# A second Strassen level for three products of the first GEMM: what it does to a TensorE-bound kernel

## The chip, the cores and the metric

The kernel runs on one core of a Trainium2 chip. The metric is the device time of one execution in microseconds (us); smaller is better. The kernel before measured 664.18 us (median of three runs, 664.06 to 664.48). A 2% rule decides "faster", "same" and "slower". A program on one core has no second die to compare with.

## The reference

A retention layer, an ELU and two matrix products, all in float32:

```python
state = gamma[None, :, None, None] * state + np.einsum('bhd,bhe->bhde', k[:, :, t], v[:, :, t])
y[:, :, t] = scale * np.einsum('bhd,bhde->bhe', q[:, :, t], state)
# ... y (4 x 8 heads x 768 x 64) becomes x, 3072 tokens x 512
h = x @ w_in                                             # 512 -> 2048, "first GEMM"
g = np.where(h > 0.0, h, np.exp(np.minimum(h, 0.0)) - 1.0)   # ELU
return (g @ w_out).astype(np.float32)                    # 2048 -> 512, "second GEMM"
```

## The kernel before

The 3072 tokens go through in six blocks of 512. Block 0 uses plain GEMMs. Blocks 1 to 5 use Strassen's algorithm: seven products M1 to M7 in place of eight. The first GEMM runs it for each of four quarters n of the output rows, and the products are summed in PSUM banks a, b and d. From block 2 on, the second GEMM has a second Strassen level: each of its seven products is again made of seven small ones ("a quadruple" gives four output quarters). Between the products of the second GEMM stand bursts of small 64x64 matmuls: the retention of the next block.

The ELU of a 128x512 tile is two ScalarE (ACT) instructions and one VectorE (DVE) instruction. The DVE part is put off until the next ELU is issued:

```python
def elu(g, h):
    r = epool.tile([P, 512], FP32, name="r", tag="r")
    nc.scalar.activation(r, h, AF.Relu, scale=-1.0)
    nc.scalar.activation(r, r, AF.Exp, scale=-1.0)
    flush()                                    # the DVE ends still put off
    later.append(lambda: nc.vector.scalar_tensor_tensor(g, r, -1.0, h, ALU.add, ALU.max))

def strassen(product, use, between):           # one quarter of the first GEMM
    # ...
    pa = bank("a");  product(1, pa, True);  m1 = kept(pa)          # kept: copy on ACT
    yield
    pb = bank("b");  product(2, pb, True);  use("C11", plus(pb, m1))   # plus: sum on DVE
    yield
    product(6, pa, False);  u2 = kept(pa)
    yield
    pd = bank("d");  product(7, pd, True)
    yield
    product(5, pa, False);  u4 = kept(pa);  use("C22", plus(pd, u4))
    yield "gap"
    product(3, pa, False);  use("C12", pa)
    yield
    product(4, pd, False);  h = plus(pd, u2)
    yield "last"
    use("C21", h)
```

The second GEMM's second level follows the same pattern with 128 columns. Two things in it matter later: `copy` is on ACT, `add` on DVE, and in the traces both engines work through their instructions in the order in which they are issued (in the trace of after, ACT starts the copy of a product whose slot ended at 277.78 us only at 280.44, behind two ELUs issued ahead of it; in that of e1_elus_behind, DVE stands idle for 1.46 us in front of one sum, and the sums behind it come later; both are shown below):

```python
def inner(j):                                  # one product of the second GEMM
    # ...
    pa = bank("a")[:, 0, 0:P];  product(j, 1, pa, True);  m1 = copy(pa)
    pb = bank("b")[:, 0, 0:P];  product(j, 2, pb, True);  add(res[:, 0, 0], pb, m1)
    yield
    product(j, 6, pa, False);  u2 = copy(pa)
    pd = bank("d")[:, 0, 0:P];  product(j, 7, pd, True)
    yield
    product(j, 5, pa, False);  add(res[:, 1, 1], pd, copy(pa))
    # ... products 3 and 4
```

Of the kernel before, what the change touches and what calls it, by code (L numbers as in the profile page):

```python
# [2 lines left out]

# [5 lines left out]
FP32 = mybir.dt.float32  # L9
# [7 lines left out]
def kernel(  # L17
# [3 lines left out]
    w_bits: bass.AP,  # L21
    scratch: bass.AP,
    scratch2: bass.AP,
    out: bass.AP,
    dims,
):



# [74 lines left out]



    w_a = [const.tile([P, 2, 2, 2, P], FP32, name=f"w_a{n}") for n in range(NQ)]
    w_b = [const.tile([P, 2, 2, 2, P], FP32, name=f"w_b{n}") for n in range(NQ)]
    w_s = [const.tile([P, 3, 2, 2, P], FP32, name=f"w_s{n}") for n in range(NQ)]
    NPIECE = 2 * NQ + NF  # L110
    staged, prepared, decoded = [], [], []

# [109 lines left out]


    xb = const.tile([P, 4, TB], FP32, name="xb")
    xt = [const.tile([P, 2, TH], FP32, name=f"xt{n}") for n in range(4)]
    carry = [const.tile([P, HP, D], FP32, name=f"carry{n}") for n in range(2)]
    held = {}

# [138 lines left out]
        while later:  # L367
            later.pop(0)()

    def elu(g, h):  # L370

        r = epool.tile([P, 512], FP32, name="r", tag="r")
        nc.scalar.activation(r, h, AF.Relu, scale=-1.0)  # L373
        nc.scalar.activation(r, r, AF.Exp, scale=-1.0)  # L374
        flush()
        later.append(lambda: nc.vector.scalar_tensor_tensor(g, r, -1.0, h, ALU.add, ALU.max))  # L376

    def plain_first():

# [167 lines left out]
                scratch2[j - 1, :, 1024 * k : 1024 * k + 1024], x.rearrange("p k f d -> p (k f d)")  # L547
            )

    def second(tb):  # L550
        def product(j, ps, begin):
            ws = fetched.pop((tb, j))
            for f in range(NF):
                for d in range(2):
                    nc.tensor.matmul(  # L555
                        ps[:, d, :], lhsT=ws[:, 2 * d + f // 4, f % 4, :], rhs=gq[INPUT2[j]][:, f, :],
                        start=(begin and f == 0 and d == 0), stop=(f == NF - 1), skip_group_check=True,
                    )
            at = ORDER2.index(j) + 3
            if j in (2, 6):  # L560
                next_input(j)
            combine_w_out(j, ws)
            if at < 7:
                fetch(tb, ORDER2[at])

        def use(name, h):
            r, t = int(name[1]) - 1, int(name[2]) - 1
            if name == "C12":
                ot = hpool.tile([P, 2, TH], FP32, name="h", tag="h")
                nc.scalar.copy(ot, h)  # L570
                h = ot
            nc.sync.dma_start(out[tb, r, t].rearrange("p d c -> p (d c)"), h.rearrange("p d c -> p (d c)"))

        return strassen(product, use, None)
# [1 line left out]


    RING = 11
    USE = [(1, k) for k in (1, 2, 6, 7, 5)]
    for at in range(1, 7):  # L580
        j, before = ORDER2[at], ORDER2[at - 1]
        USE += [(j, 1), (j, 2), (before, 3), (before, 4), (j, 6), (j, 7), (j, 5)]
    USE += [(4, 3), (4, 4)]
    to_fetch = [(tb, j, k) for tb in range(2, NTB) for j, k in USE]
    small_w = []

    def fetch_small():
        if not to_fetch:
            return
        tb, j, k = to_fetch.pop(0)  # L590
        t = ring.tile([P, 4, P], FP32, name="wq", tag="wq")
        if k in (1, 2, 4):
            q = 4 * SLOT[j] + {1: 0, 2: 1, 4: 3}[k]
            nc.sync.dma_start(t.rearrange("p f d -> p (f d)"), scratch[q])
        else:
            n = {5: 0, 6: 1, 7: 2, 3: 3}[k]
            nc.sync.dma_start(t.rearrange("p f d -> p (f d)"), scratch2[j - 1, :, 512 * n : 512 * n + 512])
        small_w.append(((tb, j, k), t))

    def second_twice(tb, behind_last):  # L600
        quarter = lambda x, r, t: x[:, 4 * r : 4 * r + 4, P * t : P * t + P]
        ts, kept2 = {}, {}

        def inputs(j):
            x, t = gq[INPUT2[j]], tpool.tile([P, 4, 4, P], FP32, name="ts", tag="ts")
            b11, b12, b21, b22 = (quarter(x, a, b) for a in range(2) for b in range(2))
            sub = lambda o, x, y: nc.vector.tensor_tensor(out=o, in0=x, in1=y, op=ALU.subtract)
            sub(t[:, 0], b12, b11)
            sub(t[:, 1], b22, t[:, 0])
            sub(t[:, 2], b22, b12)  # L610
            sub(t[:, 3], b21, t[:, 1])
            ts[j] = {1: b11, 2: b21, 3: b22, 4: t[:, 3], 5: t[:, 0], 6: t[:, 1], 7: t[:, 2]}

        def product(j, k, ps, begin):
            name, w = small_w.pop(0)
            assert name == (tb, j, k)
            for f in range(4):
                nc.tensor.matmul(  # L618
                    ps, lhsT=w[:, f, :], rhs=ts[j][k][:, f, :], start=(begin and f == 0), stop=(f == 3),
                    skip_group_check=True,  # L620
                )
            fetch_small()
# [9 lines left out]
        def inner(j):  # L632
            pool, tag = (mpool, "m") if j in (1, 6, 7, 5) else (hpool, "h")
            res = pool.tile([P, 2, 2, P], FP32, name="res", tag=tag)
            pa = bank("a")[:, 0, 0:P]
            product(j, 1, pa, True)
            m1 = copy(pa)
            pb = bank("b")[:, 0, 0:P]
            product(j, 2, pb, True)
            add(res[:, 0, 0], pb, m1)  # L640
            yield
            product(j, 6, pa, False)
            u2 = copy(pa)
            pd = bank("d")[:, 0, 0:P]
            product(j, 7, pd, True)
            yield
            product(j, 5, pa, False)
            add(res[:, 1, 1], pd, copy(pa))
            yield
            product(j, 3, pa, False)  # L650
            nc.scalar.copy(res[:, 0, 1], pa)
            product(j, 4, pd, False)
            add(res[:, 1, 0], pd, u2)
            sum_up(j, res.rearrange("p d t c -> p (d t c)"))
# [23 lines left out]
                add(m, kept2[7], m)  # L678
                store("C21", m)

        inputs(1)
        before = iter(())
        for at, j in enumerate(ORDER2):
            cur = inner(j)
            next(cur)
            if j == 1:
                yield "tail"
            for _ in before:
                pass
            if j == 2:  # L690
                next_input(2)
            if j == 5:
                next_input(6)
            if j == 1:

                next(cur)
                yield "elu"
                next(cur)
            if at + 1 < 7:
                inputs(ORDER2[at + 1])  # L700
            else:
                behind_last()
            if j != 1:
                next(cur)
                next(cur)
            before = cur
            yield j
        for _ in before:
            pass


    prepare(2)
# [51 lines left out]
            for _ in combine_w_in(0):  # L764
                pass
    combine_x()
    for j in ORDER2[:3]:
        fetch(1, j)


    def retention_step(tb, step):
# [8 lines left out]
        elif step < 5:  # L780
            outputs_step(tb, step - 2)

    tail = iter(())
    for tb in range(1, NTB):
        more = tb + 1 < NTB
        for n in range(NQ):
            cur = first(n)
            for at in range(3):
                next(cur)

            for _ in tail:
                pass
            side = combine_w_in(n + 1) if tb == 1 and n + 1 < NQ else iter(())
            for s in cur:
                next(side, None)
                if s == "gap":
                    break
            for _ in side:
                pass
            tail = cur  # L800
            if more:
                load((tb + 1) * CPB + n)
                scale_v((tb + 1) * CPB + n)
        if tb == 1:
            cur = second(tb)
            next(cur)
            next(cur)
            for _ in tail:
                pass
            flush()  # L810
            for step, s in enumerate(cur):
                retention_step(tb + 1, step)
            combine_x()
            tail = iter(())
            early.close()
            ring = ctx.enter_context(tc.tile_pool(name="ring", bufs=RING))
            tpool = ctx.enter_context(tc.tile_pool(name="tpool", bufs=2))
            for _ in range(RING):
                fetch_small()
        else:  # L820
            cur = second_twice(tb, combine_x if more else lambda: None)
            next(cur)
            for s in tail:
                if s == "last":
                    break
            next(cur)
            for _ in tail:
                pass
            flush()
            for step, j in enumerate(cur):  # L830

                if step > 0:
                    retention_step(tb + 1, step - 1)
                if j == ORDER2[-1]:
                    break
            tail = cur
    for _ in tail:
        pass

# [45 lines left out]
```

## Time and profile before

| | before |
|---|---|
| time, median of 3 | 664.18 us |
| span of the profiled run | 658.9 us |
| PE (TensorE) busy | 637.3 us, 97% |
| DVE / ACT / POOL busy | 66% / 35% / 4% |
| one product of 256 columns, start to start | 1.727 us |
| one product of 128 columns, start to start | 0.893 us |
| one token block (2 to 5), start to start | 102.65 us |

The profile counts an engine as busy from an instruction's start to its end. Matmuls overlap (a product of 256 columns is shown 1.89 us long, and the next starts 1.727 us after it), so for TensorE the distance from one start to the next says more than the busy time. One more view names the limit: the chain of work that ended last, followed back through the run. Its first line gives the share of the span that each engine has in it:

```profile
PE 95%; DVE 2%; DMA 1%; issue 1%; SPq 0%; ACT 0%; DVEq 0%
```

TensorE has 95% of the chain. No other engine delays it for long.

### The profile page before, as it was taken

The page shows a single profiled execution, that of the slowest core. Times are in us where ns is not written, and L with a number is a line of the kernel's source. Part 1 is how long each engine was busy: PE and PEld are TensorE (multiplying, and loading weights), DVE is VectorE, ACT ScalarE, POOL GpSimd, SP SyncE. Part 2 cuts the span into 40 slices and gives each one's busy share as a digit, 9 for nine tenths or more (in the row PEclk, how much of TensorE's full clock was granted, in tenths as well). Part 3 has the DMA queues.
Part 4 walks back from the last instruction along what each step waited for, and adds up shares of the span by engine and source line. Part 5 has one row for each costly group of instructions (what it writes and reads, how often), then busy time and mean ns, then how long its engine had stood idle before and what let it go on. Part 6 is the DMA issues. An engine that isn't in the chain of part 4 may idle for free.

```text
span 658.9 us, 14662 instructions
## 1 busy us (share of the span) xinstructions
PE 637.3 (97%) x6144; PEld 537.5 (82%) x6144; DVE 434.7 (66%) x769; ACT 228.3 (35%) x432; POOL 23.8 (4%) x28
## 2 busy tenths in 40 slices
PE   4799999999999999999999999999999999999997
PEld 4664445458888888889999889999889999888996
DVE  5798688566757644549856457867447958355974
ACT  7477542014431002543112554111455111445211
POOL 1000100001100000200000200000100000000000
PEclk9999999999999999999999999999999999999999
DMA  8658977549114757605767703777801768200693
GB/s 342 235 166 289 343 228 232 143 133 376 72 65 160 255 211 257 254 1 174 223 206 254 251 1 95 228 228 253 301 2 42 242 206 267 96 1 20 222 305 126
DMA packets 63825, 123.64 MB, mean 188 GB/s; under 512 B 5136, under 2 KB 22544, under 8 KB 61712
## 3 DMA queue, kind: packets, MB, share of 16 engines
q1 hardware_dynamic: 63760, 122.70, 55.6%
q8 instruction: 49, 0.80, 0.5%
q14 instruction: 16, 0.13, 0.1%
HBM read 100.66 MB, written 22.02 MB: 186 GB/s over the span
## 4 chain that ended last, share of the span: by engine, by line
PE 95%; DVE 2%; DMA 1%; issue 1%; SPq 0%; ACT 0%; DVEq 0%
PE pa L497 21%; PE pa L618 15%; PE pd L497 10%; PE pd L618 8%; PE hp L396 6%; PE pb L497 5%; PE pa L410 4%; PE pa L555 4%; PE pb L618 4%; PE pd L555 2%; PE kv L287 2%; PE pb L410 2%; PE pd L410 2%; PE y L335 2%; PE sc L265 2%; PE y L311 2%
## 5 line engine op out<-in xcount | busy, mean ns | idle before, releaser
L452 DVE TENSOR_TENSOR h<-pd,m 128x512 f32<-128x512 f32 x42 | 29.1, 692 | 86.1 <-ACT m L447 68.6
L447 ACT COPY m<-pa 128x512 f32<-128x512 f32 x63 | 36.3, 577 | 109.7 <-PE pa L497 73.7
L626 ACT COPY ms<-pa 128x128 f32<-128x128 f32 x84 | 22.3, 265 | 125.3 <-PE pa L618 122.3
L374 ACT ACTIVATE r<-r 128x512 f32<-128x512 f32 x96 | 60.5, 630 | 3.0
L618 PE MATMUL pd<-ts,wq 128*128 128x128 f32 x448 | 59.9, 277 | 0.3 <-DVE res L630 0.3
L618 PE MATMUL pa<-ts,wq 128*128 128x128 f32 x448 | 59.2, 275 | 0.0
L373 ACT ACTIVATE r<-h 128x512 f32<-128x512 f32 x60 | 37.9, 631 | 57.2 <-DVE h L452 57.2
L618 PEld LDWEIGHTS pd<-ts,wq 128*128 128x128 f32 x448 | 54.5, 192 | 1.2 <-DVE res L630 0.9
L618 PEld LDWEIGHTS pa<-ts,wq 128*128 128x128 f32 x448 | 54.8, 192 | 0.2
L618 PE MATMUL pa<-gC,wq 128*128 128x128 f32 x384 | 52.0, 278 | 0.4 <-ACT ms L626 0.4
L376 DVE SCALAR_TENSOR_TENSOR gC<-r,h 128x512 f32<-128x512 f32 x60 | 42.1, 701 | 11.3 <-ACT r L374 11.3
L618 PEld LDWEIGHTS pa<-gC,wq 128*128 128x128 f32 x384 | 47.2, 192 | 1.7 <-ACT ms L626 0.5
L239 POOL TENSOR_TENSOR kvn<-kvn,vf 128x512 f32<-128x512 f32 x20 | 21.8, 1089 | 455.7 <-DMA kvn<-in_qkv_dram 455.7
L497 PE MATMUL pa<-xb,w_s 128*128 128x256 f32 x160 | 37.8, 379 | 0.0
L497 PE MATMUL pa<-xb,w_a 128*128 128x256 f32 x160 | 37.8, 379 | 0.0
L497 PE MATMUL pa<-xt,w_s 128*128 128x256 f32 x160 | 37.8, 379 | 0.0
L497 PE MATMUL pb<-xb,w_a 128*128 128x256 f32 x160 | 37.8, 379 | 0.0
L497 PE MATMUL pd<-xt,w_s 128*128 128x256 f32 x160 | 37.8, 379 | 0.0
L497 PE MATMUL pa<-xt,w_b 128*128 128x256 f32 x160 | 37.8, 379 | 0.0
L497 PE MATMUL pd<-xt,w_b 128*128 128x256 f32 x160 | 37.8, 379 | 0.0
L630 DVE TENSOR_TENSOR res<-pd,ms 128x128 f32<-128x128 f32 x56 | 16.1, 287 | 28.8 <-PE pd L618 26.3
L497 PEld LDWEIGHTS pb<-xb,w_a 128*128 128x128 f32 x160 | 30.4, 190 | 4.1
(121 smaller groups left out, 1092.7 us busy)
## 6 DMA issues: line engine op xcount, KB each, us to landing
wq<-scratch_dram SPq DMA_DIRECT2D x196, 256.0 KB, 4.0
wraw<-in_w_dram SPq DMA_DIRECT2D x16, 1024.0 KB, 6.0
qk<-in_qkv_dram SPq DMA_DIRECT2D x24, 512.0 KB, 8.7
kvn<-in_qkv_dram SPq DMA_DIRECT2D x24, 512.0 KB, 9.4
scratch_dram<-so SPq DMA_DIRECT2D x22, 512.0 KB, 3.4
ws<-scratch_dram SPq DMA_DIRECT2D x7, 1024.0 KB, 7.0
scratch_dram<-w_s SPq DMA_DIRECT2D x8, 512.0 KB, 7.3
out_dram<-res SPq DMA_DIRECT2D x12, 256.0 KB, 3.4
```

Source lines behind the costliest of these rows:

```text
L239: eng.tensor_tensor(out=kv[:, 1], in0=kv[:, 1], in1=vf[:, i].unsqueeze(2).to_broadcast([C, H, D]), op=ALU.mult)
L373: nc.scalar.activation(r, h, AF.Relu, scale=-1.0)
L374: nc.scalar.activation(r, r, AF.Exp, scale=-1.0)
L376: later.append(lambda: nc.vector.scalar_tensor_tensor(g, r, -1.0, h, ALU.add, ALU.max))
L396: nc.tensor.matmul(hp, lhsT=w[n][:, fi, j // 2, j % 2, :], rhs=xb[:, j, :], start=(j == 0), stop=(j == 3))
L410: nc.tensor.matmul(ops[d], lhsT=wo[:, row, d * P : (d + 1) * P], rhs=g_plain[row * NF + f], start=(f == 0 and row == 0), stop=(f == NF - 1 ...
L447: nc.scalar.copy(m, ps)
L452: nc.vector.tensor_tensor(out=h, in0=ps, in1=m, op=ALU.add)
L497: nc.tensor.matmul(ps[:, fi, :], lhsT=w[:, fi, j2, :], rhs=x[:, j2, :], start=(begin and fi == 0 and j2 == 0), stop=(j2 == 1), skip_group_ ...
L555: nc.tensor.matmul(ps[:, d, :], lhsT=ws[:, 2 * d + f // 4, f % 4, :], rhs=gq[INPUT2[j]][:, f, :], start=(begin and f == 0 and d == 0), sto ...
L618: nc.tensor.matmul(ps, lhsT=w[:, f, :], rhs=ts[j][k][:, f, :], start=(begin and f == 0), stop=(f == 3), skip_group_check=True,)
L626: nc.scalar.copy(m, ps)
```

## The change

In blocks 2 to 5 the products M2, M3 and M7 of the first GEMM are taken over all four quarters at once and split by a second Strassen level: 3 x 7 small products of 128 columns replace 3 x 4 products of 256. The intent is to save TensorE work. M1 of all four quarters comes in front, then M2, M3 and M7 with their small products, then M6, M5 and M4 of the quarters. A sum is taken on DVE right behind its product, and the DVE ends of up to three ELUs may be put off, so that they come between. The new weight combinations are made once on POOL in block 1 and go to DRAM. The core of the diff (cuts marked with ..., comments added here):

```diff
-    def elu(g, h):
+    def elu(g, h, depth=1, then=None):
-        r = epool.tile([P, 512], FP32, name="r", tag="r")
+        r = epool.tile([P, 512], FP32, name="r", tag="r", bufs=3)
...
-        flush()
-        later.append(lambda: nc.vector.scalar_tensor_tensor(g, r, -1.0, h, ALU.add, ALU.max))
+        while len(later) >= depth:
+            later.pop(0)()
+        later.append(last)
...
+    def combine_small(j):
+        t = stage.tile([P, 4, 4, P], FP32, name="wi", tag="stage")
...
+        tt = lambda o, x, y, op: nc.gpsimd.tensor_tensor(out=o, in0=x, in1=y, op=op)
+        tt(s1, a21, a22, ALU.add)
+        tt(s2, s1, a11, ALU.subtract)
+        tt(s3, a11, a21, ALU.subtract)
+        tt(s4, a12, s2, ALU.subtract)
+        nc.sync.dma_start(scratch3[j - 1], t.rearrange("p k f d -> p (k f d)"))
...
+    def first_twice(tb, j):
...
+        pa = full(bank("a"))
+        product(1, pa, True)
+        m1 = lift(pa)                        # copy on ACT
+        yield
+        pb = full(bank("b"))
+        product(2, pb, True)
+        plus(0, 0, pb, m1)                   # sum on DVE
+        product(6, pa, False)
+        u2 = lift(pa)
+        pd = full(bank("d"))
+        product(7, pd, True)
+        m7 = lift(pd)
+        yield
+        product(5, pa, False)
+        plus(1, 1, pa, m7)
...
+        for at, j in enumerate(TWICE):           # TWICE = [2, 3, 7]
+            cur = first_twice(tb, j)
+            next(cur)
+            next(tail, None)
+            if at == 2:
+                first_end(1, "C11", qa[1])()     # sum on DVE, ELU on ACT
+                first_end(2, "C11", qa[2])()
+            next(cur)
+            for _ in tail:
+                pass
+            if at > 0:
+                pop()
+                first_end((0, 0, 3)[at], "C11", qa[(0, 0, 3)[at]])()
...
+        order = (6, 0), (6, 1), (5, 0), (4, 0), (5, 1), (6, 2), (4, 1), (6, 3), (5, 2), (4, 2), (5, 3)
...
+        next(sec)                            # products 1 and 2 of the second GEMM, and their sum
+        pop()
+        ends.pop(0)()
+        part(4, 3)                           # M4 of quarter 3, and the C21 sum
+        pop()
+        next(sec)                            # products 6 and 7
+        ends.pop(0)()
+        flush()
```

## The prediction

> **What bounds the kernel now.** I read the page's busy shares first, then the waits of PE, then PE's order of time, then stretches by stage.
>
> ```profile
> PE 637.3 (97%) x6144; PEld 537.5 (82%) x6144; DVE 434.7 (66%) x769; ACT 228.3 (35%) x432; POOL 23.8 (4%) x28
> ```
>
> ```profile
> PE sc L265 <- DMA qk<-in_qkv_dram: 8.9, 2, 7.5
> PE pa L385 <- DVE xb L342: 2.8, 2, 1.4
> ```
>
> PE is busy 97% of the span. Its two largest waits lie before the first 40 us are over, where this change does nothing. To learn what a busy PE is worth I took starts, not durations:
>
> ```profile
> 293.04 1.89 PE L497 MATMUL pd<-xt,w_s 128*128 128x256 f32 x8
> 294.76 1.89 PE L497 MATMUL pa<-xt,w_b 128*128 128x256 f32 x8
> ...
> 305.46 1.06 PE L618 MATMUL pb<-gC,wq 128*128 128x128 f32 x8
> 306.35 1.06 PE L618 MATMUL pa<-gC,wq 128*128 128x128 f32 x8
> ```
>
> Each row is one product of four written matmuls (two records each). A product with 256 columns starts 1.727 us before the next (several rows averaged), one with 128 columns 0.893 us. So half the columns cost 0.893/1.727 = 0.517, not 0.5.
>
> ```profile
> 353.25:399.20 45.95, 45.95 (x223) 40.68 (x222) 21.28 (x34) 22.15 (x39) 4.49 (x4) 1.00 0.40 137
> 399.20:455.90 56.70, 55.76 (x877) 54.12 (x876) 44.96 (x89) 11.42 (x34) 0.00 (x0) 1.00 0.68 211
> ```
>
> These are the first and second half of one token block (columns: stretch, PE, weight loads, DVE, ACT, POOL, clock, DMA share, GB/s). In the first GEMM PE never stops, while DVE and ACT are less than half busy. A block has 28 first-GEMM products x 1.727 = 48.4 us, 49 second-GEMM products x 0.893 = 43.8 us, and some 10.5 us of retention: 102.7 us, and the blocks start 102.65 us apart. There is nothing left to save but PE work.
>
> [...] A record here takes 1.727/8 = 216 ns and 0.893/8 = 112 ns[...]. [...] a product that accumulates on a bank must wait until the copy out of that bank is done. The trace before shows such a wait bare, with nothing put between:
>
> ```profile
> 651.28 1.06 PE L618 MATMUL pa<-ts,wq 128*128 128x128 f32 x8
> 652.37 0.27 ACT L626 COPY ms<-pa 128x128 f32<-128x128 f32 x1 [1.52 <-PE pa L618]
> 652.69 1.16 PE L618 MATMUL pa<-gC,wq 128*128 128x128 f32 x8 [0.35 <-ACT ms L626]
> ```
>
> The product's slot ends at 651.28 + 0.89 = 652.17; ACT starts 0.20 later; PE starts 0.05 after ACT ends. [...] Before, a DVE operation beside a running POOL one took 0.84 instead of 0.68 us: too little to count.
>
> **The change part by part.** In the four blocks 2 to 5, M2, M3 and M7 of the first GEMM (over all four quarters n) become 7 products of 4 small matmuls each.
> - Removed per block: 12 products x 1.727 = 20.72 us. Added: 3 x 7 x 0.893 = 18.76 us. PE gains 1.97 us per block, 7.9 us in all. Records of PE rise from 6144 to 6144 + 4 x 3 x (56 - 32) = 6432. This is a floor: 664.2 - 7.9 = 656.3 if PE stays as dense.
> - DVE gets 100 more operations (built program: 871 against 771): sums land by addition in their place instead of accumulating in PSUM, plus input combinations. A 128x512 operation is followed after 0.60 us when independent, 0.71 when it needs the one before. Some 17 of 0.60 and 8 small ones make about +12 us of DVE per block: off the path on average (66% busy), not locally.
> - ACT has 434 instructions as before, in another order. POOL gets 12 operations of about 1.09 us (13 us, once, in block 1) for new weight combinations, which go to DRAM and come back as 48 more ring tiles of 256 KB. The ring is 11 deep, the first-GEMM stage had a DMA share of 0.40, and no weight wait of PE exists before: hidden. In block 1 the second GEMM's first 1 MB weight tile is now fetched only behind that POOL work; from 166 us (end of the weight combinations on DVE) + 13 + 7 (landing of such a tile) it is there at 186, needed at 190.7. Near, but hidden; I allow 0.5 us.
>
> **New waits, worked out by hand from the orders of the engines.** Set 0 at the start of a block; the small products of M2, M3, M7 follow four 1.727 products and two left over.
> (a) During M7, PE must wait at its fifth product until ACT has copied the third out of the same bank. ACT stands in order behind two whole ELUs (quarters 1 and 2 of C11), and these behind the ELU of quarter 0. Chain: the last product of M2 ends at 18.52; +0.20 copy starts, +0.58; DVE sum 0.03 + 0.69; ACT Relu and Exp 0.04 + 0.66 + 0.63; DVE ELU end 0.04 + 0.60, a PSUM sum 0.60, the sum of quarter 1 0.69; ACT 0.04 + 0.66 + 0.54 + 0.66 + 0.54, then the copy 0.57 and 0.05 to PE: 26.3. PE is there at 24.77 (7 more products of 0.893). It waits 1.6 us.
> (b) At the end of M7 the seventh product follows after 0.89 us a DVE read (0.20 + 0.69 + 0.05): 0.05.
> (c) The twelve large products M6, M5, M4 take 20.7 us; DVE has about 37 operations of 0.60 to 0.71 there, some 23 to 24 us including the products of the second GEMM put between. It keeps up until C21 of quarter 3: its sum starts at about 23.1 on that stage's clock and the second GEMM's product on the same bank is due at 23.4: wait 0.4. Behind it the second GEMM's second input needs the last ELU end at about 26.9, when PE arrives at 26.5, but only for its third matmul: nearly nothing.
> Sum of waits 2.0 per block, 8.0 in four; 664.2 - 7.9 + 8.0 + 0.5 = 664.8. But every wait of this sum is a difference of close times, the waits can only be got wrong to the small side in (c), and a few tenths less in each step of (a), which has eleven, would halve it. I take 1.4 per block: 664.2 - 7.9 + 5.6 + 0.5 = 662.4.
>
> **Rivals.**
> - *The work shows in full.* PE stays dense and all waits hide behind neighbours: 656 to 657. For it: before, no ELU delays PE at all, and the change plainly orders sums to avoid waits. Against it: the ACT order in (a), where 2.4 us of ELUs stand directly ahead of a copy with only two small products (1.79 us) to cover it.
> - *DVE becomes the bound of M6, M5, M4.* If its operations cost 0.69 instead of 0.60 each there (many depend on the one before), 37 x 0.09 = 3.3 us more per block reach PE as waits on banks and on the second GEMM's inputs: 4 x 3.3 = 13 us, so 676. Against: runs of independent operations are seen at 0.60, and DVE waits for PE several times in that stage, which absorbs some.
> - *Weights come late* (ring or first 1 MB tiles): a few us once, 665 to 668. Against: slack of some 5 us and the low DMA share.
>
> **Range and chances.** The floor of 656.3 is firm, since the product times are measured. Upwards, (a) and (c) in full plus a late weight tile give 668. Central 662.4, eight in ten within 657 to 667.5. Over 2% faster means below 651: impossible but for an unseen saving. Over 2% slower means above 677: the whole of the DVE rival.
>
> **What would show it right or wrong.** Right: 6432 PE records, PE busy near 630 us, one wait of PE on ACT's 128x512 copy in each of four blocks of over 1 us, inside the M7 products and behind two Relu/Exp pairs; a smaller wait on DVE at the pd bank where the second GEMM begins. First GEMM stage of a block shorter than before by less than 1 us. Wrong: no PE wait on ACT (then 656 to 658), or PE waits all through the M6/M5/M4 stage on DVE (then 670 and more), or small products in the first GEMM starting further apart than 0.893 us, which would take away the gain at its root.

## The result, and the profile after

The changed kernel measured 672.51 us (median of 4 runs, 671.29 to 673.75), the kernel before 664.33 beside it. All ratios here are the mean time of one kernel's fast runs over that of the other's in the same rounds, so they are not quite the ratios of the quoted medians. This one is 1.0109, with a 95% interval of 1.0066 to 1.0152: "same" by the 2% rule, but slower, since the interval leaves out 1, and outside the predicted range of 657 to 667.5.

The head of the page, then the waits of TensorE (columns: engine, instruction and line, what it waited for, us in total, times, longest), of the kernel after:

```profile
PE 636.6 (95%) x6432; PEld 542.8 (81%) x6432; DVE 490.3 (73%) x869; ACT 227.8 (34%) x432; POOL 43.7 (7%) x40
```

```profile
PE sc L269 <- DMA qk<-in_qkv_dram: 9.6, 2, 7.5
PE pa L688 <- ACT m L698: 5.5, 4, 1.5
PE pd L777 <- DVE gC L742: 2.9, 4, 1.1
PE pa L398 <- DVE xb L346: 2.8, 2, 1.4
PE y L315 <- issue: 2.5, 2, 1.9
PE sc L269 <- issue: 1.7, 1, 1.7
```

The first and fourth line stood before the change too. Two of these lines are new: a wait on the ACT copy in the small products (L688), four times, and a wait on a DVE sum at bank d where the second GEMM begins (L777), four times. The "issue" lines are waits for nothing that the profile shows; more on them below. Among the smaller lines left out, a second DVE sum at bank d (`res`, L777) has 1.2 us in three waits, where it had 0.3 before. The chain that ended last, of the kernel after:

```profile
PE 74%; DVE 15%; ACT 6%; issue 3%; DMA 1%; SPq 0%; DVEq 0%
```

TensorE's share fell from 95% to 74%; DVE and ACT, together 2% before, now have 21% of the chain that sets the end.

**Where the time went.** I added TensorE's start-to-start times by line, stage by stage. The last column is a second profile of the unchanged kernel (run b_again below), which shows what comes and goes without any change:

| TensorE time, us | before | after | difference | before, once more |
|---|---|---|---|---|
| retention and its bursts | 64.2 | 66.4 | +2.2 | 67.1 |
| block 0, plain GEMMs | 111.4 | 114.2 | +2.8 | 113.1 |
| first GEMM, blocks 1 to 5 | 241.8 | 243.5 | +1.8 | 241.8 |
| second GEMM, block 1 | 49.3 | 49.4 | +0.1 | 49.3 |
| second GEMM, blocks 2 to 5 | 180.2 | 185.7 | +5.4 | 180.3 |

The sum of the differences before rounding is 12.2 us; the two spans, 658.86 and 671.24, differ by 12.4 (the rest is what follows the last matmul). The last three rows repeat to 0.1 us in the unchanged kernel, the first two don't: its second profile is 4.6 us longer than its first, all of it in these two rows. So the change itself cost some 7.3 us (1.8 + 0.1 + 5.4), and the profile of before that I had predicted from was one of its short executions.

In the first GEMM the twelve products taken out took 12 x 4 x 1.727 = 82.9 us. The small ones in their place took 83.5 instead of the 21 x 4 x 0.893 = 75.0 predicted. The saving went whole into waits and the restarts behind them. Block 1 took 1.1 us more, which gives +1.8 with rounding (83.5 - 82.9 + 1.1).

The first new wait, in order of time in block 2 of the kernel after (columns: start, us, engine, line, operation, out<-in, count, and in brackets the idle time before it and what ended that; other rows cut):

```profile
278.06 0.63 ACT L379 ACTIVATE r<-gC 128x512 f32<-128x512 f32 x1 [1.49 <-DVE gC L742]
...
278.68 1.06 PE L688 MATMUL pa<-xb,wq 128*128 128x128 f32 x8
278.73 0.63 ACT L380 ACTIVATE r<-r 128x512 f32<-128x512 f32 x1
279.26 0.61 ACT L379 ACTIVATE r<-gC 128x512 f32<-128x512 f32 x1
...
279.91 0.63 ACT L380 ACTIVATE r<-r 128x512 f32<-128x512 f32 x1
...
280.44 0.57 ACT L698 COPY m<-pa 128x512 f32<-128x512 f32 x1
...
281.06 1.16 PE L688 MATMUL pa<-ts,wq 128*128 128x128 f32 x8 [1.33 <-ACT m L698]
```

The copy that TensorE needs (280.44) stands on ACT behind two whole Relu and Exp pairs (278.06 to 280.44). TensorE has one small product left (278.68, over at 279.57 on its 0.893 us grid) and then stands still until the copy is done. It is the chain (a) of the prediction. The profile gives the wait as 1.33 us from the modelled end of the matmul before; counted on the grid, as the prediction counted, it is 281.06 - 279.57 = 1.49 us, in place of 1.6.

In block 1 a second thing shows, at the start of POOL's weight combinations:

```profile
168.42 0.69 DVE L444 TENSOR_TENSOR w_b<-w_b 128x512 f32<-128x512 f32 x1
168.51 1.72 POOL L634 TENSOR_TENSOR wi<-w_s 128x512 f32<-128x512 f32 x1 [83.11 <-DVE w_s L444]
169.14 1.64 DVE L444 TENSOR_TENSOR w_s<-w_b,w_a 128x512 f32<-128x512 f32 x1
...
170.31 1.59 POOL L634 TENSOR_TENSOR wi<-wi,w_s 128x512 f32<-128x512 f32 x1
170.82 1.64 DVE L444 TENSOR_TENSOR w_s<-w_a,w_s 128x512 f32<-128x512 f32 x1
```

With both of its inputs in SBUF, DVE takes 1.64 us here beside a POOL operation in place of 0.69 (a sum with one input in PSUM takes 0.68 beside POOL at 172.38), and POOL's twelve operations take 1.27 to 1.73 where a POOL operation of this size took 1.04 in the kernel before: each takes longer beside the other. The twelve last from 168.5 to 187.4, 18.9 us where 13 were counted, and so the first weight tile is fetched at 187.8 instead of the 179 that I had worked out. I also put one wait of TensorE on DVE (0.57 us) down to it; no run takes that wait alone.

The start, last, in the table of stretches (columns as in the prediction's table of stretches; the last but two is the granted clock). First the kernel before, then after:

```profile
7.00:41.00 34.00, 27.65 (x562) 23.89 (x563) 26.39 (x46) 17.88 (x35) 0.00 (x0) 1.00 0.67 262
```

```profile
7.00:41.00 34.00, 26.60 (x547) 23.02 (x548) 22.85 (x43) 14.52 (x31) 0.00 (x0) 0.90 0.61 236
```

The clock of the kernel after fell to half for 6.83 us at 19.6 us, so less was done in the same stretch. The kernel before had no such stretch in this profile, and one of 3.41 us in the next. A group of 16 matmul records of 128x256 (L398, from 20.76 us) that ran mostly at half clock took 6.50 us; the same group took 3.72 in the kernel before. Between the first rise of the clock and the last matmul every half-clock stretch in the traces is 3.41 us, twice that (6.83 us in this one), or (at the 13 us wait of e4_weights_dve, below) four times that, and of the profiles without padding (the small matmuls added below) some have one and some have none.

### The profile page after: what moved, and what is told of

It is laid out like the page before. It is cut to its first block, busy times and chain, and to the rows that moved or that the text cites. A ratio compares the mean times of both kernels' runs of the same rounds, so it can differ in the third digit from the quotient of the medians.

```text
span 671.2 us, 15515 instructions
## 1 busy us (share of the span) xinstructions
PE 636.6 (95%) x6432; PEld 542.8 (81%) x6432; DVE 490.3 (73%) x869; ACT 227.8 (34%) x432; POOL 43.7 (7%) x40
## 4 chain that ended last, share of the span: by engine, by line
PE 74%; DVE 15%; ACT 6%; issue 3%; DMA 1%; SPq 0%; DVEq 0%
PE pa L777 13%; PE pd L777 7%; PE qa L734 6%; PE hp L409 6%; PE pa L688 5%; PE pa L568 4%; PE pa L423 4%; DVE gC L742 4%; DVE gC L383 3%; PE pa L510 3%; ACT r L380 3%; PE pb L777 3%; ACT r L379 3%; DVE ts L645 3%; PE pd L688 2%
## 5 line engine op out<-in xcount | busy, mean ns | idle before, releaser
L777 PE MATMUL pd<-ts,wq 128*128 128x128 f32 x448 | 60.2, 277 | 4.5 <-DVE gC L742 2.9
L777 PEld LDWEIGHTS pd<-ts,wq 128*128 128x128 f32 x448 | 54.4, 192 | 6.3 <-DVE gC L742 3.6
L777 PE MATMUL pa<-ts,wq 128*128 128x128 f32 x448 | 59.3, 275 | 0.0
L379 ACT ACTIVATE r<-gC 128x512 f32<-128x512 f32 x64 | 40.0, 625 | 50.8 <-DVE gC L742 44.9
L777 PEld LDWEIGHTS pa<-ts,wq 128*128 128x128 f32 x448 | 54.8, 192 | 0.4 <-ACT ms L785 0.3
L777 PE MATMUL pa<-gC,wq 128*128 128x128 f32 x384 | 52.0, 278 | 0.4 <-ACT ms L785 0.4
L777 PEld LDWEIGHTS pa<-gC,wq 128*128 128x128 f32 x384 | 47.2, 192 | 1.7 <-ACT ms L785 0.5
L383 DVE SCALAR_TENSOR_TENSOR gC<-r,gC 128x512 f32<-128x512 f32 x64 | 44.5, 710 | 3.7 <-ACT r L380 3.7
L742 DVE TENSOR_TENSOR gC<-qa,gC 128x512 f32<-128x512 f32 x48 | 31.1, 682 | 10.1 <-ACT gC L698 10.1
L645 DVE TENSOR_TENSOR ts<-gC,ts 128x512 f32<-128x512 f32 x48 | 33.7, 703 | 0.8
L645 DVE TENSOR_TENSOR ts<-gC 128x512 f32<-128x512 f32 x48 | 32.9, 685 | 0.0
L698 ACT COPY m<-pa 128x512 f32<-128x512 f32 x24 | 13.9, 580 | 53.9 <-PE pa L688 53.9
L688 PE MATMUL pa<-ts,wq 128*128 128x128 f32 x192 | 26.1, 279 | 5.5 <-ACT m L698 5.5
L423 PE MATMUL pa<-gC,w_s 128*128 128x512 f32 x64 | 30.6, 600 | 0.0
L734 PE MATMUL qa<-xt,w_b 128*128 128x256 f32 x128 | 30.2, 379 | 0.0
L734 PE MATMUL qa<-xt,w_s 128*128 128x256 f32 x128 | 29.6, 379 | 0.0
L734 PE MATMUL qa<-xb,w_a 128*128 128x256 f32 x128 | 28.8, 379 | 0.0
```

What stands on the lines that cost most here:

```text
L379: nc.scalar.activation(e, h, AF.Relu, scale=-1.0)
L383: nc.vector.scalar_tensor_tensor(g, e, -1.0, h, ALU.add, ALU.max)
L423: nc.tensor.matmul(ops[d], lhsT=wo[:, row, d * P : (d + 1) * P], rhs=g_plain[row * NF + f], start=(f == 0 and row == 0), stop=(f == NF - 1 ...
L645: sub = lambda o, x, y: nc.vector.tensor_tensor(out=o, in0=x, in1=y, op=ALU.subtract)
L688: nc.tensor.matmul(ps[:, f, :], lhsT=lhs[f], rhs=xs[j][k], start=(begin and f == 0), stop=True, skip_group_check=True,)
L734: nc.tensor.matmul(ps[:, fi, :], lhsT=w[:, fi, j2, :], rhs=x[:, j2, :], start=(j in (1, 4) and fi == 0 and j2 == 0), stop=(j2 == 1), skip_ ...
```

## The experiments

Eighteen runs were made, in five calls. All gave correct results, and every run was classed as fast. Each call measured the kernel before again on the same chip. "Ratio" is always against that.

| run | median, us (range) | before beside it | ratio (95%) |
|---|---|---|---|
| e1_elus_behind | 663.84 (662.87-665.49) | 662.67 | 1.0015 (0.9971-1.0058) |
| e2_c21_first | 671.87 (668.68-674.11) | 662.67 | 1.0130 (1.0078-1.0182) |
| e4_weights_dve | 689.28 (685.93-689.56) | 662.67 | 1.0379 (1.0322-1.0436) |
| b_again | 664.35 (661.77-667.00) | 662.67 | 1.0020 (0.9967-1.0073) |
| e6_53_last | 670.60 (667.94-671.78) | 664.10 | 1.0086 (1.0049-1.0124) |
| e7_warm_64 | 672.80 (670.85-675.51) | 664.10 | 1.0128 (1.0090-1.0166) |
| e8_warm_32 | 666.37 (665.17-670.11) | 664.10 | 1.0040 (0.9993-1.0088) |
| b_warm_64 | 663.89 (662.61-666.72) | 664.10 | 0.9997 (0.9960-1.0034) |
| e9_own_bank | 665.09 (662.86-668.41) | 662.60 | 1.0036 (1.0009-1.0064) |
| e10_own_bank_32 | 662.38 (659.33-663.73) | 662.60 | 0.9984 (0.9959-1.0010) |
| b_warm_32 | 661.53 (658.75-663.72) | 662.60 | 0.9976 (0.9949-1.0002) |
| a_warm_32 | 669.83 (667.73-671.08) | 662.60 | 1.0101 (1.0079-1.0123) |
| e13_sum_later_d | 662.96 (660.31-664.61) | 664.72 | 0.9969 (0.9945-0.9994) |
| e11_sum_later | 662.33 (661.86-665.40) | 664.72 | 0.9967 (0.9945-0.9988) |
| e12_sum_later_32 | 660.38 (658.55-663.16) | 664.72 | 0.9930 (0.9907-0.9953) |
| e14_sum_later_d_32 | 660.16 (656.91-662.68) | 664.72 | 0.9922 (0.9894-0.9949) |
| e14_again | 660.89 (657.88-662.51) | 663.38 | 0.9958 (0.9926-0.9990) |
| b_warm_32_again | 662.56 (660.31-664.65) | 663.38 | 0.9987 (0.9958-1.0017) |

### The ELUs in front of M7's copies

```diff
-            if at == 2:
-                first_end(1, "C11", qa[1])()
-                first_end(2, "C11", qa[2])()
             next(cur)
             for _ in tail:
                 pass
             if at > 0:
                 pop()
-                first_end((0, 0, 3)[at], "C11", qa[(0, 0, 3)[at]])()
+                for n in ((), (0,), (1, 2, 3))[at]:
+                    first_end(n, "C11", qa[n])()
```

> The changed kernel, but the ELUs of C11's quarters 1 and 2 are issued behind the copies of the M7 products instead of ahead of them. Order theory: the four PE waits on ACT's 128x512 copy (1.33, 1.33, 1.52 and 1.33 us, and some 0.2 us for the restarts) go, nothing takes their place, and the time falls by 5.5 to 6.2 us against the changed kernel, to about 666.5 us where the start runs at half clock. Rival (DVE and ACT are simply too full): the ELUs come later, the M6/M5/M4 stage starts with a longer queue, and the wait on the pd bank at the second GEMM's start grows by as much: under 2 us gained.

It held, but for a small part of the rival: the wait on bank d grew from 2.9 to 3.6 us. The four waits on the copy are gone, and the small products' sum fell from 83.5 to 76.5 us. The ratio went from 1.0109 to 1.0015 (across two calls). What stays, in the waits of TensorE of this kernel:

```profile
PE pd L777 <- DVE gC L742: 3.6, 4, 1.1
...
PE kv L291 <- issue: 2.0, 1, 2.0
```

### The C21 sum first

The part that ends in the C21 sum was put ahead of the second GEMM's first two products (the last `next(sec)` before it moved behind it), in the changed kernel as handed over.

> The changed kernel, but the last product of M4 (and with it the C21 sum of quarter 3) stands ahead of the first two products of the second GEMM instead of behind them. Order theory: the four PE waits on that sum at the pd bank (0.49, 1.09, 0.79, 0.49 us: 2.9 us) go, the time falls by 2.5 to 3.2 us. Rival (DVE is full in that stage): the wait moves to the second GEMM's second input or to its pa bank, under 1 us gained.

The rival held. The wait on bank d went, and TensorE now waits for the copy of product 1, which stands behind ELUs:

```profile
PE pa L777 <- ACT ms L785: 3.8, 5, 1.2
```

The time stayed where it was (ratio 1.0130), and the second GEMM's TensorE time too (185.1 us).

### The weight combinations on DVE

```diff
-        tt = lambda o, x, y, op: nc.gpsimd.tensor_tensor(out=o, in0=x, in1=y, op=op)
+        tt = lambda o, x, y, op: nc.vector.tensor_tensor(out=o, in0=x, in1=y, op=op)
```

> The changed kernel, but the twelve weight combinations of block 1 run on DVE instead of POOL. [...] two-input DVE operations beside POOL's took 1.6 to 1.8 us instead of 0.69 and delayed PE by about 1 us in block 1 (one wait of 0.57 us and a late start of the second GEMM of about 0.4 us): those operations are back at 0.69, and 0.8 to 1.2 us are gained. Rival: DVE is delayed by its own 12 more operations (8.4 us) and PE waits as much or more.

A miss, and a bad one. The twelve operations then stand in DVE's queue behind block 1's other work, and the second GEMM's first weight tile is fetched behind their results:

```profile
PE pa L568 <- DMA ws<-scratch_dram: 13.0, 1, 13.0
```

One part of the expectation did come true: without POOL beside them, the two DVE operations that took 1.64 us take 0.69 again, so it was POOL's work that stretched them:

```profile
169.05 0.69 DVE L444 TENSOR_TENSOR w_s<-w_b,w_a 128x512 f32<-128x512 f32 x1
169.78 0.69 DVE L444 TENSOR_TENSOR w_s<-w_a,w_s 128x512 f32<-128x512 f32 x1
```

Here the price of running beside POOL was smaller than the price of making weights late (13.0 us of waiting). What POOL's work in block 1 costs by itself is not measured by this run: both went into it together. The trace of after puts it near 1 us (an estimate: block 1 took 1.1 us more in the first GEMM, 0.57 of it in that wait).

### The kernel before once more

> The kernel before, unchanged, to see the start in each of its runs. If the half clock at the start (6.8 us of it in the profile of the changed kernel, none in that of before, worth 3.7 us) comes by chance, some runs here have a clock below 1 and take 3 to 4 us longer (one run of before took 668.3). If the changed program causes it, all runs here have clock 1.000 and 664 us, and all runs of the changed kernel's variants have clocks near 0.995.

Its profile had the half-clock stretch in the start and 7.1 us of issue waits over 0.4 us, against 3.4 in the first profile. Both losses come with the unchanged kernel too.

### The issue waits and the start

In every trace, each issue wait over 0.4 us after the first 40 us begins at a TensorE instruction whose index (all of TensorE's instructions counted from the first) is 193 modulo 256. These waits are 0.4 to 3.1 us each, and 1.5 to 7.1 us in sum in a run of some 660. The instruction queue of the DMA brings packets of 0.84 MB / 51 = 16 KB; the trace of after has 13,111 TensorE records, which is 257 for each of its 51 packets. One such wait, in the trace of e11_sum_later (below): after 94 matmuls in 1.6 us, TensorE stands for 3.07 us, while a 16 KB packet that starts at 322.53 takes 1.86 us:

```profile
321.06 1.62 PE L291 MATMUL kv<-kvn 64*64 64x64 f32 x94
...
325.75 0.79 PE L291 MATMUL kv<-kvn 64*64 64x64 f32 x34 [3.07 <-issue]
```

My reading is that TensorE had run out of instructions: that a burst of 64x64 matmuls uses up a packet faster than the next one comes. TensorE starts again 1.36 us after this packet's end; what it waits for in that time the trace doesn't show. In the lists of waits taken from these traces nearly all of them stand in the bursts of 64x64 matmuls, up to 3.1 us (e11_sum_later); the longest at a large product is 0.6 us (`pb`, L777, in e4_weights_dve and e9_own_bank).

To test it, small matmuls of zeros that nothing reads were put ahead of everything, where TensorE waits for the first data anyway. A written one is four TensorE instructions, so 64 shift everything by one whole packet and 32 by half a packet. The base of e7 and e8 is e6_53_last (told in the next part).

```diff
+    warm = carry[1][:, 0, :]
+    nc.gpsimd.memset(warm, 0.0)
+    for b in range(4):
+        unused = ps_r.tile([P, 2, HP, D], FP32, name="unused", tag="r")
+        for i in range(16):                  # 8 in the kernels with 32
+            r = slice(b % 2 * D, b % 2 * D + D)
+            o = slice(i % 2 * D, i % 2 * D + D)
+            nc.tensor.matmul(unused[o, 0, 0, :], lhsT=warm[r], rhs=warm[r], start=True, stop=True, ...)
```

> The kernel e6_53_last with 64 small matmuls of zeros (256 TensorE instructions, weight loads counted) ahead of everything, in the 7.5 us in which TensorE waits for the first data; nothing reads them. Theory of the start: the clock has risen before the real work, so no half clock after 12 us and the start of the hp stage comes 1 to 3.5 us earlier than without. The positions of the instruction fetches stay as they are (256 is a whole fetch), so the issue waits stay at the same instructions. Expected: median 1 to 3 us under e6_53_last. Rival: the clock falls later in the start all the same[...]: no difference within 1 us.

> As e7_warm_64 with half as many small matmuls: 128 TensorE instructions, half a fetch, so every later instruction fetch falls at another place of the program. Theory of position: the issue waits of TensorE over 0.4 us move to other instructions (index still 193 modulo 256) and their sum changes by more than 1 us either way from e7_warm_64, and the median with it. Rival: the waits come from the bursts of small matmuls wherever the fetch falls; sum and median within 1 us of e7_warm_64.

> The kernel before with the same 64 small matmuls ahead: if the start costs both kernels the same, it too gains 1 to 3 us against the unchanged kernel before, and the difference to e7_warm_64 stays what e6_53_last has to the kernel before.

The theory of the start fell: with 64 small matmuls ahead the kernel was no faster (672.8 beside 670.6), the kernel before gained nothing from them either (0.9997), and in e7's profile, with the small matmuls from 2.9 to 8.9 us, the clock rose for the first time at 25.75 us (at 14.3 in that of the kernel before and at 16.2 in that of after, both without any). The theory of position held in direction: all runs of e8 (665.17 to 670.11) lie under all of e7 (670.85 to 675.51), and in their profiles the issue waits over 0.4 us sum to 5.9 and 1.5 us, at other instructions, still at 193 modulo 256. But the pair differs in more than the shift. The 64 matmuls of e7 are still running when the first data are there, so that its real work starts at 8.24 us, that of e8 at 7.52; and the first 512-column product of block 0 starts at 43.92 and 38.92 us. So 5.0 of the 8.9 us between the two spans lie in the start, and whether the padding or chance put them there is not shown.

The same shift elsewhere:

> The kernel before with the same 32 small matmuls. If the positions of the instruction fetches cost any kernel of this program alike, it too changes, by up to 3 us either way, since its unshifted profiles show 3 to 7 us of issue waits; b_warm_64, which keeps the positions, did not change. If it doesn't change by over 1 us, the positions are special to the changed kernel.

> The changed kernel as it was handed over, with the 32 small matmuls ahead and nothing else. Theory of position: its issue waits (5.2 us over 0.4) fall to 1.5 to 2.5 us, and its half clock in the start goes in most runs, so 2 to 6 us under the changed kernel's 672.5 (666.5 to 670.5), while its four waits on the copy in M7 (5.5 us) and on bank d (2.9) stay. Rival: all of the loss lies in these waits, and nothing changes (over 671).

The kernel before gained 0.24%, and 0.13% when it was repeated; both intervals take in 1. In the changed kernel the ratio went from 1.0109 to 1.0101 across two calls, which shows no gain: its 669.8 us lies in the expected range, but the kernel before was 1.7 us faster in that call too. In the three other pairs of one call (e9 and e10, e13 and e14, e11 and e12) the shifted kernel was 0.4 to 0.5% faster, with e10 short of its expected 657 to 661. In these pairs' profiles the issue waits fell by 1.2 to 3.7 us, while that product of block 0 started from 0.1 us later to 3.8 us earlier. So the padding was worth up to some 3 us here, in some variants; how much of it comes from the places of the issue waits and how much from the start, no run separates. Both must be kept in mind when two kernels of different length are compared. Neither explains the loss: a_warm_32 still loses 1.0% to the kernel before.

### The wait at the start of the second GEMM

First, another order: the last M4 part ahead of the last M5 part.

```diff
-        order = (6, 0), (6, 1), (5, 0), (4, 0), (5, 1), (6, 2), (4, 1), (6, 3), (5, 2), (4, 2), (5, 3)
+        order = (6, 0), (6, 1), (5, 0), (4, 0), (5, 1), (6, 2), (4, 1), (6, 3), (4, 2), (5, 2), (4, 3)
...
+        part(5, 3)                           # between products 2 and 6 of the second GEMM
...
-        part(4, 3)
...
-        flush()
+        pop()
```

> The kernel with the C11 ELUs behind the M7 copies (663.8 us), and the last M4 part of the first GEMM now taken before the last M5 part, so that a whole M5 part of 1.7 us and the two C ELU ends of M5 come between its vector sum and the first product of the second GEMM that needs bank d again. My theory: the four waits on bank d for the C21 sum (3.6 us there, 1.09 each at most) go, and no other wait of more than 0.3 us in each block takes their place; the profile's wait of TensorE on the C21 sum falls under 0.5 us, and the median comes to 659.5 to 661.5, ratio to the kernel before 0.993 to 0.998. Rival: the wait moves once more (to the copy of the second product's bank a on ScalarE behind the ELUs of M5, as when the M4 part went ahead of both products), 663 to 667, with a sum of waits over 0.5 us on ms or pa of 3 us or more.

The rival held, and it was worse than the rival: the second GEMM took 191.1 us of TensorE, and the wait is back on the copies:

```profile
PE pa L777 <- ACT ms L785: 5.7, 5, 1.3
```

Next, another bank, on top of e1_elus_behind:

```diff
-            pd = bank("d")[:, 0, 0:P]
+            pd = ps_r.tile([P, 2, TH], FP32, name="pr", tag="r")[:, 0, 0:P] if j == 1 else bank("d")[:, 0, 0:P]
```

> The kernel with the C11 ELUs behind the M7 copies, and product 7 of the second GEMM's first quadruple in a bank of the rotating pool (one that the first GEMM has long left) instead of bank d. In that kernel's trace the wait of 1.09 us on bank d in the third block ends 0.15 us after the copy of product 6, so product 5 could start about 0.9 us earlier. Theory: the sum of waits on the C21 sum (3.6 us) goes, and at most 0.2 us per block comes back on the copy of product 6; the time comes out 2 to 3.5 us under e1_elus_behind, 660 to 662 us, ratio to the kernel before 0.993 to 0.998. Rival, which has held twice: the wait moves whole to a copy on ScalarE behind an ELU (sum of waits on ms of 3 us or more) and the time stays at 663 to 666.

> As e9_own_bank with the 32 small matmuls (128 TensorE instructions) ahead of everything. Theory of position: as with e8_warm_32, TensorE's issue waits fall to under 2 us in sum and the half clock in the start doesn't come back in most runs; 1 to 5 us under e9_own_bank (657 to 661). Rival: the 6 us between e7_warm_64 and e8_warm_32 were chance of those runs; within 1 us of e9_own_bank.

The waits on bank d went, and of what they cost nearly nothing came out (second GEMM 187.3 to 186.4 us; e1's included about 1 us of half clock). Two others had taken their place:

```profile
PE pb L777 <- DVE gC L383: 1.9, 4, 0.5
...
PE pa L777 <- ACT ms L785: 1.4, 4, 0.4
```

Three times the wait had moved. What the traces of after, e1 and e9 share is one DVE instruction in front of which DVE stands idle for 1.2 to 1.5 us in each of the four blocks; in e6 for 0.95 us. (In e2 it is 0.12 us at most; there TensorE waits for the copy itself.) In e1_elus_behind, block 2:

```profile
299.65 0.61 ACT L379 ACTIVATE r<-gC 128x512 f32<-128x512 f32 x1
300.29 0.63 ACT L380 ACTIVATE r<-r 128x512 f32<-128x512 f32 x1
300.83 0.25 ACT L785 COPY ms<-pa 128x128 f32<-128x128 f32 x1
301.11 0.29 DVE L789 TENSOR_TENSOR res<-pb,ms 128x128 f32<-128x128 f32 x1 [1.46 <-ACT ms L785]
...
302.64 0.68 DVE L742 TENSOR_TENSOR gC<-pd,m 128x512 f32<-128x512 f32 x1
...
303.38 1.16 PE L777 MATMUL pd<-ts,wq 128*128 128x128 f32 x8 [1.09 <-DVE gC L742]
```

DVE, the busiest helper of this stretch, stands idle for 1.46 us in front of a sum that nobody needs soon (`res`): it waits for the copy of product 1, and that copy stands on ACT behind ELUs. All DVE work behind it, the C21 sum too, comes that much later: the C21 sum starts 1.47 us after the slot of its product ends (299.44 + 1.727 = 301.17, the product's start from the same trace). The test is to move this one sum behind the C21 sum:

```diff
+    first_sum = []
...
             product(j, 2, pb, True)
-            add(res[:, 0, 0], pb, m1)
+            if j == 1:
+                first_sum.append(lambda: add(res[:, 0, 0], pb, m1))
+            else:
+                add(res[:, 0, 0], pb, m1)
...
         part(4, 3)
+        first_sum.pop(0)()
         pop()
```

> e1_elus_behind (bank d kept) with one DVE instruction moved: the sum of products 1 and 2 of the second GEMM's first quadruple, which in every trace since the change stands on DVE ahead of the C21 sum and there waits 1.46 us for the copy of product 1 (the copy stands on ScalarE behind ELU pairs), now comes behind the C21 sum. Theory: this idle stretch of DVE is the root of the late C21 sum, whatever bank TensorE then waits for; the idle stretch goes, the C21 sum comes 1.2 us earlier, the four waits on bank d (3.6 us) fall to under 0.5 in sum and the second GEMM's TensorE start-to-start sum from 187.3 to 183 or less. Rival: DVE simply has too much work here (99 per cent busy), and the wait stays or moves: sum of TensorE's waits there over 2.5 us, second GEMM 186 or more.

> The same move in e9_own_bank. Theory: its waits on the ELU end before product 2 of the next quadruple (4 x 0.48) and on the copy of product 6 (4 x 0.35) go, second GEMM 186.4 to 183.0 or less, the time 2.5 to 3.5 us under e9_own_bank. Rival: no change within 1 us.

> e11_sum_later with the 32 small matmuls ahead, the best version there is by the theory: e10_own_bank_32 measured 662.4 beside 662.6 for the kernel before, so 659 to 660 beside it, ratio 0.993 to 0.996, an interval that leaves out 1. Rival: 661.5 to 663, nothing gained.

> e13_sum_later_d with the 32 small matmuls ahead: by the theory within 1 us of e12_sum_later_32, as the bank was never the cause; by the rival over 1.5 us slower than it, as the wait on bank d is still there.

The theory held. The same place in e13_sum_later_d:

```profile
303.92 0.69 DVE L742 TENSOR_TENSOR gC<-pd,m 128x512 f32<-128x512 f32 x1
...
304.53 0.28 DVE L791 TENSOR_TENSOR res<-pb,ms 128x128 f32<-128x128 f32 x1
304.73 1.89 DVE L383 SCALAR_TENSOR_TENSOR gC<-r,gC 128x512 f32<-128x512 f32 x3
...
304.97 1.06 PE L779 MATMUL pd<-ts,wq 128*128 128x128 f32 x8
```

The idle stretch is gone, the C21 sum comes first, 0.20 us after the slot of its product (301.99 + 1.727 = 303.72), and TensorE runs into bank d without a wait. The second GEMM fell from 187.3 to 181.8 us, with an own bank from 186.4 to 182.2, so the bank was not the cause. The ratio fell from 1.0015 to 0.9969, and from 1.0036 to 0.9967, each across two calls. The move was tested on e1 and e9 only, not on the changed kernel as handed over, whose trace shows the same idle stretches (1.22, 1.46, 1.46 and 1.22 us). The claim that DVE simply had too much work here is refuted by the same runs: e13 has the same 869 DVE instructions.

With the shift by half a packet this makes the best version: 0.9922 of the kernel before. To tell whether the shift alone would do:

> e14_sum_later_d_32 once more, on the same chip as the padded kernel before: 0.992 of the unpadded kernel before (0.989 to 0.995), and 0.994 to 0.996 of the padded one, so that what is left of the gain without the padding is 2.5 to 4 us. Rival: the padded kernel before gains as much as it, and the two are within 1 us.

> The kernel before with the same 32 small matmuls, beside e14_again: 0.9976 of the unpadded one again, within its interval of 0.995 to 1.000.

The version won again (0.9958, the interval leaves out 1), but only by 660.89 to 662.56 against the shifted kernel before, less than expected, and the intervals of the two ratios overlap. It beats the kernel before in both calls, by 0.4 to 0.8% (2.8 to 5.2 us). Without any shift, e13 and e11 beat it too, by 0.3%, with intervals that leave out 1. How the gain of the shifted version divides between change and padding stays open to some 2 us.

## Why the prediction was wrong

By its own steps:

- **The floor: right.** 6432 records came out, the small products start 0.893 us apart where nothing holds them, and with the waits removed they take 76.5 us (75.0 by the prediction). Only the busy sum of TensorE missed: 636.6 us, not near 630. It adds durations, which overlap (1.89 us against 1.727 from start to start) and stretch at half clock (6.50 us against 3.72), and I did not follow it further.
- **(a), the copy behind two ELUs: right in kind, place and number of times.** It measured 1.33, 1.33, 1.52 and 1.33 us by the profile, 1.49, 1.49, 1.69 and 1.49 on the grid of starts, where the hand count gave 1.6. In all, the small products lost 8.5 us in four blocks, where 6.6 were counted for (a) and (b). Run e1_elus_behind shows (a) as the cause: the products gave back 7.0 us. The other 1.5 us I did not follow.
- **(c), the start of the second GEMM: the step that failed most.** It gave 0.4 us per block, 1.6 in all; the stage lost 5.4. The wait that it names, on the C21 sum at bank d, measured 0.49, 1.09, 0.79 and 0.49 us, 2.9 in all. Of the rest, which it had taken for "nearly nothing", another DVE sum at that bank has 0.9 more than before and an issue wait 0.5; I did not follow what remains. The step counted DVE's operations by their durations. It left out the order of DVE's instructions, though the prediction had counted ACT's in order in (a): one early sum, waiting for a copy behind ELUs, held everything behind it for 1.2 to 1.5 us. Runs e13 and e11 show that: with the sum moved, the stage comes to 181.8 us, so 3.9 of the 5.4 are gone. The last 1.6 us over the 180.2 before stay open.
- **"I take 1.4 per block": the shading was wrong.** The count gave 2.0 and was cut because "every wait of this sum is a difference of close times". The waits lost 8.5 + 5.4 = 13.9 us in four blocks, 3.5 per block. There was no reason for the errors to go one way down: the prediction itself says that (c) can only be too small. And to halve (a), each of its eleven steps need be less by only 0.07 us, not by "a few tenths", which would undo the wait altogether; the measured wait came out about 0.1 us from the count.
- **"Too little to count": wrong in size.** DVE beside POOL took 1.64 us, not 0.84, in block 1, where POOL works without a pause. The case in the kernel before that I had looked at overlapped only in part: POOL's operation (376.44, 1.04 us) ends 0.29 us after that of DVE starts (377.19). Block 1 lost 1.1 us, of which the trace shows 0.57 as a wait on DVE. The 0.5 us for late weights was not used: the tile came just in time here, and 0.2 to 1.6 us late in the profiles of five variants (e2, e8, a_warm_32, e14 and its repeat).
- **Not in the prediction at all: the run-to-run part.** The profile of before, 658.9 us, was a short one. The half-clock stretch at the start and the issue waits differ from run to run, with 4.6 us between two profiles of the same kernel. This does not excuse the miss, since the medians too differ by 8.2 us.

Put together, starting from the median before and with the terms as the profiles give them: 664.2 - 7.9 (saved) + 8.5 (small products) + 5.4 (second GEMM) + 1.1 (block 1) = 671.3. Measured 672.5. The rest of 1.2 us is inside what chance moves. Against the prediction's 662.4, (c) makes 3.8 us of the miss, the shading 2.6, (a) and (b) 1.9 and block 1 0.6.

Of the rivals, none came about as written. "Waits all through the M6/M5/M4 stage on DVE" was announced as the sign for 670 and more; the time came, the sign did not. TensorE waited on DVE mainly at one place per block, behind one misplaced instruction.

## What to carry to other kernels

A saving on the busiest engine is worth only what the engines beside it can hand over in time (here 7.9 us of saving met 13.9 us of loss), so write out their queues in order, with the waits in them, before counting their durations. When a wait moves from bank to copy to sum each time it is removed, look at the engine that releases it for an instruction that stands idle in front of needed work, and move that one. Compare kernels by several runs each and keep in mind that a kernel of another length can have its issue waits at other instructions (128 instructions more or less, between e7 and e8: 5.9 and 1.5 us in sum).
